# A table of turns for the engines' order up to the spectra, one weight tile loaded from ScalarE's queue, and the last stores of v on two queues

## The chip, the cores and the metric

The kernel runs on one core of one Trainium2 chip. The metric is the device time of one execution in microseconds (us), and lower is better. Engines are named as the profile names them: PE is TensorE, DVE is VectorE, ACT is ScalarE, POOL is GpSimd, and SP is SyncE, which here only issues DMAs. All arithmetic is in float32; where a matmul needs more than one pass allows, its operands are split into a high part (`..h`) and a low part (`..l`).

## The reference

The inputs are a sequence `u` of 2048 rows with 448 channels, the parameters of a diagonal state-space layer (S4D) with 256 modes for each channel, and the three matrices of a gated linear unit (GLU), 448 to 1792 and back. The row normalisation of `u` goes into both branches, and the output is the sum of `u` and the two.

```python
xn  = (u - mean(u)) / sqrt(var(u) + 1e-5)            # per row, L=2048, D=448
# S4D branch: a kernel K[d, l] for each channel, then a convolution of length 2L by FFT
dt  = exp(log_dt);  A = -exp(log_A_real) + 1j*A_imag
C   = (C_real + 1j*C_imag) * dt[:, None]
P   = exp((A*dt[:, None])[:, :, None] * arange(L))   # D x 256 x L
K   = 2 * einsum("dn,dnl->dl", C, P).real
y   = irfft(rfft(xn^T, 2L) * rfft(K, 2L), 2L)[:, :L]^T + xn * D_skip
# GLU branch, F = 1792
g   = (sigmoid(xn @ w_gate) * (xn @ w_up)) @ w_down
out = u + y + g
```

## The kernel before, in words

Two Python generators emit the program, and a driver takes turns between them by shares of planned work, so that the convolution's small operations lie among the GLU's matmuls. `conv()` holds the S4D branch and `glu()` the GLU.

`glu()` works on two halves of 1024 rows, with 14 tiles of 128 hidden columns in groups (`FCH`). For each tile f the weights come by DMA into `wraw` (`w_load`, L646 and L648, six DMAs: for each of two matrices three blocks of 128 rows, and the last 64 rows in two parts). ACT rounds them to `wh` (L763) and DVE takes the rest, `wl` (L767). There is a single buffer `wraw`, so the load of the next tile can start only when both have read it. `gate` makes the products `gu` (PE, L712, four banks of PSUM for `gu`, `po` and others together), `th` on ACT (L720), `hf` on DVE (L723), `hh` on ACT (L728), `hl` on DVE (L730). With `dh` (ACT, L793) and `dl` (POOL, L794) the down product `po` follows on PE (L826), and DVE adds it to `acc` (L831). Some weights are stored for the second half (`wt_d`, `dt_d`, L784).

`conv()` first normalises, makes the first stage of the transform of xn (`x_spec`), and prepares the S4D parameters (`prep`), whose phases it stores to memory (`phu_d`, `phv_d`, `phh_d`, L390). Then comes the kernels' stage, `kgen`, in 56 chunks of 8 channels (the loop variable `cn`). A chunk has these steps:

- `ahead`: phases `ph` are loaded (L489), PE multiplies them out to `tr` (L539), and ACT turns them into cosines and sines `S` (L547 to L550, the last of which, L550, depends on L547).
- `powers`: DVE makes the powers `pm` of the modes' decay, each from the one before it (L453), with three operations of ACT (L446, and L456 twice); a set serves 8 chunks.
- `magnitudes`: POOL spreads the powers to tables `me` and `mf` (L505, L517), and ACT squares part of them (L530).
- DVE multiplies `me` and `mf` with `S` to the factors `Et` (L604 and L605) and `Ft` (L606).
- PE sums the modes, `ko` (L620). After four chunks, ACT copies the sums to `ks` (L633), PE makes the first stage of their transform, `kp` and `kq` (L565), ACT copies these to `sk` (L571) and issues their store to `sk_d` (L572).

After that the spectra: for 17 steps, the kernels' and xn's first stages are loaded (`skl`, `sx`), PE finishes the transforms (`sp`, L912), DVE multiplies them (`yy`), `back` turns the product to `pv` on PE (L939), ACT copies it to `vt` (L945), and SP stores it to `v_d` (L957). `turned` loads it in another order (`vp`, L963), and `last` makes the output (L974). The sums `acc` of the first half go to memory (`acc_d`) and come back as `ac` (L1017).

What sets the order before: the Tile scheduler puts instructions of an engine in order by priority. `tc.high_priority` (called `hp`) moves an operation ahead, and `tc.issue_after(x)` holds one back until x has been placed:

```python
with tc.issue_after(glu_mm[0].ins):       # PE: L285, L434, L620, L565
with tc.issue_after(fts[0].ins) if behind else nullcontext():   # powers: L453, L456
with tc.issue_after(mls[0].ins) if mls else nullcontext():      # magnitudes on POOL
with tc.issue_after(sins[0].ins) if sins else nullcontext():    # squares on ACT
```

Each engine then works through its list strictly in order; a waiting instruction holds up everything behind it.

## Time and profile before

| what | value |
|---|---|
| time, median of 3 runs | 729.61 us (727.99 to 733.26) |
| profiled execution | 730.14 us |
| its span | 728.4 us (1.74 us of the time lie around it) |
| mean granted TensorE clock | 0.978 of full speed |
| instructions in the span | 19114 |

The span runs from the first to the last instruction in the trace, and all positions in the text are counted from its start. Busy shares are means over the span; an engine's idle time has in brackets the instruction or the transfer that ended it. A row of a timeline joins equal instructions that follow one another (`x3`), and its length is then that of all of them. Starts of pipelined instructions overlap the ends of those before them by some tenths of a microsecond.

### The profile page before, as it was taken

The numbers are of one execution on the slowest core, as the hardware profiler recorded it, in microseconds if no ns is written. First come the engines' busy times: TensorE is split into PE (matmuls) and PEld (weight loads), VectorE is DVE, ScalarE is ACT, GpSimd is POOL, SyncE is SP. The second block draws the span as 40 slices with busy tenths as digits, with TensorE's granted clock in tenths as the row PEclk, the third lists the DMA queues.
The fourth block names the chain that finished last, engine by engine and source line by source line (L and its number), as shares of the span: only waits on it lengthen the run. The fifth ranks groups of instructions, "written<-read, shape, count | busy, mean of one in ns | idle before, by whom it ended". The sixth has DMA issues, their size and how long they took to land.

```text
span 728.4 us, 19114 instructions
## 1 busy us (share of the span) xinstructions
PE 682.1 (94%) x7789; PEld 537.9 (74%) x7789; DVE 567.6 (78%) x777; ACT 421.3 (58%) x651; POOL 379.4 (52%) x425
## 2 busy tenths in 40 slices
PE   2997899997998999999999999999999999998996
PEld 1775688786876788666777887888877787776785
DVE  5699997699999999999589988987866555565544
ACT  3645455678677788898397687776742222322320
POOL 2111018699888688788556865776845001351002
PEclk9998899999999999998999999999999999999999
DMA  9936328524414445354853242232269999999845
GB/s 205 233 100 185 103 80 253 170 96 166 161 51 134 168 148 172 99 184 139 247 165 132 59 146 93 73 110 68 74 159 249 287 232 225 236 239 234 189 131 162
DMA packets 92711, 115.72 MB, mean 159 GB/s; under 512 B 12432, under 2 KB 81040, under 8 KB 92368
## 3 DMA queue, kind: packets, MB, share of 16 engines
q1 hardware_dynamic: 83328, 94.15, 47.8%
q10 hardware_dynamic: 6752, 14.69, 6.4%
q0 software_dynamic: 2544, 5.67, 3.2%
q8 instruction: 61, 1.00, 0.6%
q14 instruction: 26, 0.21, 0.1%
HBM read 69.70 MB, written 44.76 MB: 157 GB/s over the span
## 4 chain that ended last, share of the span: by engine, by line
PE 60%; DVE 14%; DMA 11%; ACT 6%; issue 4%; POOL 3%; SPq 2%; ACTq 0%; DVEq 0%; POOLq 0%
PE gu L712 25%; PE po L826 14%; PE ko L620 6%; PE sp L912 5%; PE tr L539 4%; PE pv L939 3%; DVE Ft L606 2%; DVE Et L605 2%; DVE Et L604 2%; DMA acc_d<-acc 1%; DMA tb<-in_c_tab_dram 1%; POOL me L517 1%; DVE hl L730 1%; DMA xe<-in_A_u_dram 1%; DMA sx<-x_d 1%
## 5 line engine op out<-in xcount | busy, mean ns | idle before, releaser
L517 POOL TENSOR_TENSOR me<-me,pm 128x32 f32<-128x32 f32 (+1 forms) x168 | 145.6, 866 | 88.0 <-DVE Et L605 75.5
L517 POOL TENSOR_TENSOR mf<-mf,pm 128x64 f32<-128x64 f32 (+1 forms) x112 | 118.6, 1059 | 4.9
L712 PE MATMUL gu<-xh,wh 128*128 128x512 f32 x336 | 101.9, 410 | 1.4 <-ACT xh L220 1.4
L712 PE MATMUL gu<-xh,wl 128*128 128x512 f32 x336 | 95.7, 392 | 0.0
L712 PE MATMUL gu<-xl,wh 128*128 128x512 f32 x336 | 95.1, 390 | 0.0
L826 PE MATMUL po<-dh,hh 128*128 128x448 f32 (+1 forms) x227 | 87.4, 385 | 4.5 <-DVE acc L831 2.5
L604 DVE TENSOR_TENSOR Et<-me,S 128x1024 f32<-128x1024 f32 x56 | 82.3, 1469 | 9.0 <-ACT S L550 6.7
L605 DVE TENSOR_TENSOR Et<-me,S 128x1024 f32<-128x1024 f32 x56 | 79.5, 1420 | 8.6 <-ACT me L530 8.4
L606 DVE TENSOR_TENSOR Ft<-mf,S 128x1024 f32<-128x1024 f32 x56 | 80.2, 1432 | 7.0 <-ACT S L550 4.3
L826 PE MATMUL po<-dl,hh 128*128 128x448 f32 (+1 forms) x227 | 85.1, 375 | 0.0
L826 PE MATMUL po<-dh,hl 128*128 128x448 f32 (+1 forms) x227 | 84.2, 372 | 0.0
L547 ACT ACTIVATE S<-tr 128x1024 f32<-128x1024 f32 x56 | 57.8, 1032 | 43.5 <-PE tr L539 36.2
L712 PEld LDWEIGHTS gu<-xh,wh 128*128 128x128 f32 x336 | 62.4, 193 | 20.4 <-issue 4.9
L728 ACT CAST hh<-hf 128x512 fp32r<-128x512 f32 x56 | 35.0, 625 | 73.3 <-DVE hf L723 59.6
L620 PEld LDWEIGHTS ko<-Et,Ft 128*32 128x32 f32 x3584 | 54.9, 112 | 27.5 <-issue 17.2
L712 PEld LDWEIGHTS gu<-xh,wl 128*128 128x128 f32 x336 | 63.3, 189 | 15.1 <-DVE pl L313 0.7
L620 PE MATMUL ko<-Et,Ft 128*32 128x64 f32 x3584 | 65.1, 225 | 9.3 <-DVE Ft L606 4.8
L712 PEld LDWEIGHTS gu<-xl,wh 128*128 128x128 f32 x336 | 63.0, 188 | 14.0 <-issue 0.7
L723 DVE SCALAR_TENSOR_TENSOR hf<-th,gu 128x512 f32<-128x512 f32 x56 | 38.1, 680 | 36.8 <-PE gu L712 26.2
L550 ACT ACTIVATE S<-S,hpi 128x1024 f32<-128x1024 f32 x56 | 65.5, 1170 | 0.0
L831 DVE SCALAR_TENSOR_TENSOR acc<-po,acc 128x448 f32<-128x448 f32 (+1 forms) x81 | 48.7, 611 | 21.0 <-PE po L826 21.0
L720 ACT ACTIVATE th<-gu 128x512 f32<-128x512 f32 x56 | 33.7, 601 | 49.2 <-PE gu L712 49.2
(198 smaller groups left out, 1311.1 us busy)
## 6 DMA issues: line engine op xcount, KB each, us to landing
sk_d<-sk ACTq DMA_DIRECT2D x14, 512.0 KB
sx<-x_d SPq DMA_DIRECT2D x32, 224.0 KB
skl<-sk_d SPq DMA_DIRECT2D x16, 448.0 KB
vp<-v_d SPq DMA_DIRECT2D x16, 448.0 KB
v_d<-vt SPq DMA_DIRECT2D x62, 112.0 KB
wt_d<-wh SPq DMA_DIRECT2D x9, 512.0 KB
wt_d<-wl SPq DMA_DIRECT2D x9, 512.0 KB
wl<-wt_d SPq DMA_DIRECT2D x9, 512.0 KB
```

The lines of the kernel that those rows point to most:

```text
L517: ins = nc.gpsimd.tensor_tensor(m[:, :, w + a : 2 * w : n], m[:, :, a:w:n], par(base + i).unsqueeze(2).to_broadcast([128, 4 * DC, w // n]) ...
L547: nc.scalar.activation(rows(cs), pv, AF.Abs)
L550: sins[:] = [nc.scalar.activation(cs, cs, AF.Sin, scale=-TWO_PI, bias=hpi)]
L604: v.tensor_tensor(Et[:, :, :, 32:64], two(me[:, :, 32:64]), S[:, 1::-1], ALU.mult)
L605: v.tensor_tensor(Et[:, :, :, 0:32], two(me[:, :, 0:32]), S[:, 1:3, :, ::-1], ALU.mult)
L606: fts[:] = [v.tensor_tensor(Ft, two(mf), S[:, 3:5], ALU.mult)]
L620: nc.tensor.matmul(ko[32 * j : 32 * j + 32, sl], Ft[:, cc, DC * h + 4 * q + j], Et[:, cc, DC * h + 4 * q + j], start=(k == 0), stop=(k == ...
L712: glu_mm[:] = [nc.tensor.matmul(ps, a_, b_, start=(n == 0), stop=(n == len(mm) - 1))]
L723: marks[1] = v.scalar_tensor_tensor(hf, th, 1.0, pgu[1], ALU.add, ALU.mult)
L826: glu_mm[:] = [nc.tensor.matmul(po[:, ds], a_[:, bs], w_[:, ds], start=(n == 0), stop=(n == 3 * fc - 1))]
L831: v.scalar_tensor_tensor(acc[:, b, ds], po[:, ds], 0.5, acc[:, b, ds], ALU.mult, ALU.add)
L912: mm = nc.tensor.matmul(to, tb[:kk, t, 64 * c : 64 * c + 64], rhs, start=True, stop=True, skip_group_check=True,)
```

## The change

There are three parts.

First, a table `TURNS` holds, for DVE, ACT, POOL and PE, the positions of instructions in the order in which the program emitted them; `0 2 1 3+2` reads: the first, the third, the second, and then two from the fourth on. After all is emitted, `in_turn` chains every instruction of an engine that the table names to the one ahead of it, without a semaphore, so that the scheduler keeps this order. The table ends where the spectra begin (about 300 us into the span). Where the program held an operation back by `issue_after` in that part, the call is now `free`, which does nothing. Second, the load of the GLU's weight tile 7 (issued at f = 6) goes out from ACT's queue in place of SP's. Third, in the very last `back`, DVE copies the second half of `vt`, and the four stores to `v_d` go out two from SP and two from ACT.

```diff
+TURNS = {
+    "DVE": """
+0 2 1 3+2 6 5 7+15 26 30 32 34 36 31 33 22 35 24 37 25 29 38 23 39+13 27 86+2 28 56 52 54+2 58 60 62 64 66 68
...
+def in_turn(tc):
+
+    info = mybir.DependencyInfo(mybir.DependencyClass.NoSync, mybir.DependencyReason.DATA)
+    traced = tc.nc.cur_bb.bb.instructions
+    for name, text in TURNS.items():
+        own = [i for i in traced if i.engine == getattr(mybir.EngineType, name)]
+        turns = []
+        for run in text.split():
+            first, _, n = run.partition("+")
+            turns += own[int(first) : int(first) + int(n or 1)]
+        for one, two in zip(turns, turns[1:]):
+            tc.add_manual_dep(two, one.name, info, reason="in_turn")
...
+    free = lambda ins: nullcontext()
...
-            with tc.issue_after(glu_mm[0].ins):
+            with free(glu_mm[0].ins):
...
-            with tc.issue_after(fts[0].ins) if behind else nullcontext():
+            with free(fts[0].ins) if behind else nullcontext():
...
-            with tc.issue_after(sins[0].ins) if sins else nullcontext():
+            with free(sins[0].ins) if sins else nullcontext():
...
-                                raws.append((w_load(f + 1), None))
+                                raws.append((w_load(f + 1, eng=nc.scalar if f == 6 else nc.sync), None))
...
-                            with hp(HP), tc.issue_after((act if f == 1 else marks)[0].ins):
+                            with hp(HP), free((act if f == 1 else marks)[0].ins):
...
-        def back(h, k, ys_):
+        def back(h, k, ys_, engs=(nc.sync, nc.sync)):
...
-                nc.scalar.copy(vt[:, i], pvs[i])
...
+                if i and engs[0] is not engs[1]:
+                    v.tensor_copy(vt[:, i], pvs[i])
+                else:
+                    nc.scalar.copy(vt[:, i], pvs[i])
+
+            pairs = [(j, i) for j in range(2) for i in range(n)]
+            for j, i in pairs if engs[0] is engs[1] else sorted(pairs, key=lambda p: p[1]):
+                k1 = k + 2 * j + i
...
+                engs[j].dma_start(to.rearrange("r w d -> w r d"), fr)
...
-        back(*prev)
+        back(*prev, (nc.sync, nc.scalar))
...
+    in_turn(tc)
```

The lines of the changed kernel stand 89 lines further down than those of the kernel before in most of the program (L453 is L542 there, L723 is L812, L831 is L920).

How this moves instructions is shown at three places. The first is DVE's order where the kernels' stage opens, about 121 to 134 us into the span of before: `pm0` are the powers, `wl_1601` is the low part of weight tile 7, `hf`, `hl` and `acc` belong to the GLU. Before:

```order
L723 SCALAR_TENSOR_TENSOR hf_1209<-th_1207,gu_1195 128x512
L730 TENSOR_TENSOR hl_1212<-hf_1209,hh_1211 128x512
L453 SCALAR_TENSOR_TENSOR pm0_1132<-W1_110 128x128
L831 SCALAR_TENSOR_TENSOR acc_102<-po_1215,acc_102 128x448
L453 SCALAR_TENSOR_TENSOR pm0_1132<-pm0_1132 128x128 x3
L767 TENSOR_TENSOR wl_1601<-wraw_1413,wh_1600 128x1024
L831 SCALAR_TENSOR_TENSOR acc_102<-po_1226,acc_102 128x448
L453 SCALAR_TENSOR_TENSOR pm0_1132<-pm0_1132 128x128
L831 SCALAR_TENSOR_TENSOR acc_102<-po_1237,acc_102 128x448
L453 SCALAR_TENSOR_TENSOR pm0_1132<-pm0_1132 128x128 x3
L831 SCALAR_TENSOR_TENSOR acc_102<-po_1248,acc_102 128x448
```

After the change, the same place:

```order
L812 SCALAR_TENSOR_TENSOR hf_1209<-th_1207,gu_1195 128x512
L542 SCALAR_TENSOR_TENSOR pm0_1132<-W1_110 128x128
L819 TENSOR_TENSOR hl_1212<-hf_1209,hh_1211 128x512
L920 SCALAR_TENSOR_TENSOR acc_102<-po_1215,acc_102 128x448
L542 SCALAR_TENSOR_TENSOR pm0_1132<-pm0_1132 128x128 x6
L856 TENSOR_TENSOR wl_1601<-wraw_1413,wh_1600 128x1024
L542 SCALAR_TENSOR_TENSOR pm0_1132<-pm0_1132 128x128 x2
L920 SCALAR_TENSOR_TENSOR acc_102<-po_1226,acc_102 128x448
L542 SCALAR_TENSOR_TENSOR pm0_1132<-pm0_1132 128x128
L920 SCALAR_TENSOR_TENSOR acc_102<-po_1237,acc_102 128x448
L920 SCALAR_TENSOR_TENSOR acc_102<-po_1248,acc_102 128x448
```

Seven of the ten powers now stand ahead of `wl_1601`, where four stood, and the other three are through one or two additions earlier.

The second place is ACT's order at the same time: `th` and `hh` are the GLU's, `GG_111` takes the prepared C, `pm0` is the powers' tile, and `wraw_1413` and `wh_1600` are weight tile 7. Before:

```order
L720 ACTIVATE th_1207<-gu_1183 128x512
L728 CAST hh_1211<-hf_1209 128x512
L436 COPY GG_111<-ko_1040 128x2x14x8
L436 COPY GG_111<-kp_1044 128x2x14x8
L446 ACTIVATE pm0_1132<-W1_110,one_74 128x128
L763 CAST wh_1600<-wraw_1413 128x1024
L456 ACTIVATE pm0_1132<-pm0_1132,one_74 128x640 x2
```

After the change:

```order
L809 ACTIVATE th_1207<-gu_1183 128x512
L535 ACTIVATE pm0_1132<-W1_110,one_74 128x128
L735 DMA wraw_1413<-in_B_w_gate_dram 128x3x128
L817 CAST hh_1211<-hf_1209 128x512
L525 COPY GG_111<-ko_1040 128x2x14x8
L737 DMA wraw_1413<-in_B_w_gate_dram 64x128
L525 COPY GG_111<-kp_1044 128x2x14x8
L737 DMA wraw_1413<-in_B_w_gate_dram 64x128
L735 DMA wraw_1413<-in_B_w_up_dram 128x3x128
L737 DMA wraw_1413<-in_B_w_up_dram 64x128 x2
L852 CAST wh_1600<-wraw_1413 128x1024
L545 ACTIVATE pm0_1132<-pm0_1132,one_74 128x640 x2
```

The powers' first operation now stands ahead of `hh_1211` and of both copies to `GG_111`, and the six DMAs of the weight load, which stood among the stores of `phv_d` and `phh_d` on SP's queue, lie between these.

The third place is ACT's order in the kernels' stage, at a copy `ks` of the modes' sums (about 172 us into the span of before). Before:

```order
L720 ACTIVATE th_2581<-gu_2525 128x512
L793 CAST dh_2593<-rd_2594 128x448
L530 ACTIVATE me0_1131<-me0_1131 128x32x16
L728 CAST hh_2585<-hf_2583 128x512
L633 COPY ks_1122<-ko_2067 128x512
L547 ACTIVATE S1_1125<-tr_2409 128x2x2x256
L548 ACTIVATE S1_1125<-tr_2409 128x2x2x256
L549 ACTIVATE S1_1125<-tr_2409 128x512
L720 ACTIVATE th_2729<-gu_2624 128x512
```

After the change:

```order
L809 ACTIVATE th_2581<-gu_2525 128x512
L882 CAST dh_2593<-rd_2594 128x448
L722 COPY ks_1122<-ko_2067 128x512
L636 ACTIVATE S1_1125<-tr_2409 128x2x2x256
L637 ACTIVATE S1_1125<-tr_2409 128x2x2x256
L817 CAST hh_2585<-hf_2583 128x512
L638 ACTIVATE S1_1125<-tr_2409 128x512
L639 ACTIVATE S1_1125<-S1_1125,hpi_72 128x2x512
L809 ACTIVATE th_2729<-gu_2624 128x512
```

The copy `ks` and two of the sines now stand ahead of `hh_2585`. PE's order in that stage has the kernels' chunks `ko` up to five GLU matmuls earlier, `tr` and `kp` up to eight; from about 310 us on DVE, ACT, POOL and PE have the order of before. On SP, besides the six DMAs, the four loads of `ac` (L1017) stand together ahead of two loads of the spectra (`skl`, `sx`), and the load of `t32` stands one place earlier.

More of the change, by code (lines that the diff above doesn't have):

```diff
@@ L54 @@
 NCH = 8
+TURNS = {
+    "DVE": """
[18 rows of a table added]
+""",
+    "Activation": """
[15 rows of a table added]
+""",
+    "Pool": """
[8 rows of a table added]
+""",
+    "PE": """
[22 rows of a table added]
+""",
+}
+def in_turn(tc):
[9 more added lines that the diff above has]
+            tc.add_manual_dep(two, one.name, info, reason="in_turn")
 def _tables():
@@ L430, in turn @@
             ps = psc[-1].tile([128, 2, 128], F32, name=("ko", "kp")[t], bufs=1)
-            with tc.issue_after(glu_mm[0].ins):
+            with free(glu_mm[0].ins):
                 for k in range(2):
@@ L444, in powers @@
         pm = pms[g % 2]
-        with tc.issue_after(behind.ins) if behind else nullcontext():
+        with free(behind.ins) if behind else nullcontext():
             nc.scalar.activation(pm[:, 0], w, AF.Identity, bias=one)
@@ L502, in magnitudes @@
             gg = GGs[0][:, 2 * b : 2 * b + 2].rearrange("p c h e -> p (c h e)")
-            with tc.issue_after(mls[0].ins) if mls else nullcontext():
+            with free(mls[0].ins) if mls else nullcontext():
                 nc.gpsimd.tensor_tensor(
@@ L515, in magnitudes @@
                     a, n = (1, 2) if m is me and i > 3 else (0, 1)
-                    with tc.issue_after(mls[0].ins) if mls else nullcontext():
+                    with free(mls[0].ins) if mls else nullcontext():
                         ins = nc.gpsimd.tensor_tensor(
@@ L613, in kgen @@
                     ko = psc[-1].tile([128, 8, 64], F32, name="ko", bufs=1)
-                with tc.issue_after(glu_mm[0].ins):
+                with free(glu_mm[0].ins):
                     for q in range(2):
@@ L635, in kgen @@
                 if cn % 4 == 2 and cn > 3 or cn + 1 == NCK:
-                    with hp(HP) if cn + 1 == NCK else tc.issue_after(glu_mm[0].ins):
+                    with hp(HP) if cn + 1 == NCK else free(glu_mm[0].ins):
                         first_stage((cn - 3) // 4 if cn + 1 < NCK else cn // 4)
@@ L676, in pair_norm @@
     def pair_norm(b, xns):
-        with hp(HP), tc.issue_after(marks[0].ins), tc.issue_after(marks[1].ins):
+        with hp(HP), free(marks[0].ins), free(marks[1].ins):
             for i in range(2):
@@ L1075, in conv @@
                     with hp(HP):
-                        with tc.issue_after(normed.ins) if q else nullcontext():
+                        with free(normed.ins) if q else nullcontext():
                             for b in range(4 * q, 4 * q + 4):
@@ L1094, in conv @@
                 preps = [prep(pst, h, srcs[h]) for h in range(2)]
-                with tc.issue_after(xls[0].ins):
+                with free(xls[0].ins):
                     for b in range(8):
@@ L1110, in conv @@
                         try:
-                            with tc.issue_after(hfs[max(0, len(hfs) - LAG)].ins):
+                            with free(hfs[max(0, len(hfs) - LAG)].ins):
                                 next(p)
```

16 lines of the change are left out of this document (6 added, 10 removed), and 62 rows, old and new, of the table TURNS.

## The prediction, before the changed kernel had run

> **What bounds the kernel now.** I read the page first, for the engines' shares, then the busy times by stretch, then the waits inside the stretch that the change rearranges, then the timelines at its two ends.
>
> ```profile
> PE 682.1 (94%) x7789; PEld 537.9 (74%) x7789; DVE 567.6 (78%) x777; ACT 421.3 (58%) x651; POOL 379.4 (52%) x425
> ```
>
> TensorE (PE) is busy for 94% of the span, so the 46 us in which it is not are nearly all that an order can win. The shares hide stages with different limits, which the next view separates. Its columns are the stretch, its length, the busy time of PE, PEld, DVE, ACT and POOL, the granted clock, the DMA share and GB/s.
>
> ```profile
> 120.00:140.00 20.00, 18.28 (x90) 16.20 (x89) 9.70 (x21) 8.32 (x14) 9.97 (x18) 1.00 0.74 233
> 140.00:300.00 160.00, 151.20 (x2203) 122.42 (x2202) 152.76 (x152) 125.60 (x183) 135.76 (x134) 0.98 0.39 130
> 345.00:545.00 200.00, 196.92 (x3003) 161.97 (x2998) 163.85 (x170) 139.43 (x202) 133.34 (x154) 1.00 0.39 121
> 545.00:680.00 135.00, 132.57 (x1033) 99.66 (x1033) 75.56 (x144) 37.48 (x72) 31.87 (x37) 1.00 1.03 243
> ```
>
> From 140 to 300 us VectorE (DVE) works 152.76 of 160 us and PE 151.20: the two run neck and neck, and PE has 8.8 us to give. From 345 on PE is busy for 98%, so what the kernel gains before 300 us is carried to the end rather than swallowed by a later wait; from 545 to 680 the DMA engines are full as well (1.03), and the bytes are the same in both kernels. The waits from 138 to 300 us (engine and line <- what ended the wait: us in total, times, longest) say what holds PE in that stage, and what holds DVE:
>
> ```profile
> PE ko L620 <- DVE Ft L606: 3.1, 4, 1.9
> PE ko L620 <- DVE Et L604: 2.9, 1, 2.9
> PE kp L565 <- ACT ks L633: 1.9, 2, 1.0
> ```
>
> ```profile
> DVE Et L604 <- ACT S L550: 3.2, 2, 2.2
> DVE Et L605 <- ACT me L530: 2.2, 5, 0.6
> ```
>
> PE loses 7.9 us to the kernels' factors (Et, Ft) and to the copy of their sums (ks). Those products come late because DVE is full, and DVE itself loses only 5.4 us to ScalarE (ACT) work that is late. An order can take away such waits; it can't shorten DVE's 152.76 us.
>
> **The opening (term 1).** The kernels' chain starts here with the powers pm on DVE (L453). The next two views are DVE's and ACT's timelines (start, us, operation, and in brackets the idle time before it and what ended it):
>
> ```profile
> 124.32 0.93 DVE L453 SCALAR_TENSOR_TENSOR pm<-pm 128x128 f32<-128x128 f32 x3
> 130.29 1.23 DVE L767 TENSOR_TENSOR wl<-wraw,wh 128x1024 fp32r<-128x1024 f32 x1 [5.04 <-ACT wh L763]
> 131.44 0.62 DVE L831 SCALAR_TENSOR_TENSOR acc<-po,acc 128x448 f32<-128x448 f32 x1
> ...
> 134.09 0.86 DVE L453 SCALAR_TENSOR_TENSOR pm<-pm 128x128 f32<-128x128 f32 x2
> ...
> 140.11 1.23 DVE L604 TENSOR_TENSOR Et<-me,S 128x1024 f32<-128x1024 f32 x1 [2.20 <-ACT S L550]
> ```
>
> ```profile
> 123.32 0.41 ACT L446 ACTIVATE pm<-W,one 128x128 f32<-128x128 f32 x1
> 129.21 1.05 ACT L763 CAST wh<-wraw 128x1024 fp32r<-128x1024 f32 x1 [5.48 <-DMA ph<-phu_d]
> 133.02 0.83 ACT L456 ACTIVATE pm<-pm,one 128x640 f32<-128x640 f32 x1 [2.76 <-DVE pm L453]
> 134.98 0.83 ACT L456 ACTIVATE pm<-pm,one 128x640 f32<-128x640 f32 x1 [1.13 <-DVE pm L453]
> ...
> 138.86 1.16 ACT L550 ACTIVATE S<-S,hpi 128x1024 f32<-128x1024 f32 x1
> ```
>
> Before, DVE does four powers (the last three in the first row), sits 5.04 us behind wl (which waits for wh, and wh for the loaded weights), and then does the last six among the acc additions. ACT's two `one`-additions (L456) wait for these, and the sines behind them (the last is L550) set the first Et at 140.11. After, three more powers, seven in all, stand ahead of wl. The six that the first L456 needs lie in the 5.04 us of idle time, so that it starts when wh ends, 129.21 + 1.05 = 130.26, not at 133.02. The second L456 needs the three that are left: wl ends at 130.29 + 1.23 = 131.52, two powers take 0.86, the acc addition that stands among them 0.62, the last power half of 0.86: 133.43 against 134.98, 1.55 earlier. From there the chain to L550 and Et has the same instructions, so **term 1 is -1.5 us**. What is late next: the chain's first tr, of which PE's timeline says:
>
> ```profile
> 132.90 0.70 PE L539 MATMUL tr<-sel,ph 128*128 128x512 f32 x2 [1.72 <-DMA ph<-phv_d]
> ```
>
> It ends at 133.60, and in the new order the first sine wants it at about 134.5 (133.43, plus 0.83 for L456 and a short square), so this wait doesn't come to bind. That PE idle time of 1.72 us I count as not won: the next po matmuls need banks that the acc additions free, and these now stand behind wl and two powers.
>
> The new ACT order puts a wait here. pm's first operation (L446), which stood behind hh and the two copies of GG, now stands ahead of them, and it overwrites memory that a store of the parameters still reads (fr to phv_d). SP's timeline gives that store and the weight load of tile 7, which moves to ACT's queue:
>
> ```profile
> 118.98 0.96 SPq L390 DMA_DIRECT2D phv_d<-fr  x1
> ...
> 125.89 1.18 SPq L648 DMA_DIRECT2D wraw<-in_B_w_up_dram  x2
> ```
>
> The store has landed no earlier than its issue ends, 119.94, and no later than 123.32, where L446 ran before without a wait; between these I take 122.5, near the later end, since the stores issued ahead of it share the DMA engines. Queued behind it on ACT are hh, both GG copies, and the six issues of the load. hh is wanted by the po matmuls, of which PE has work to 131, so a delay of a microsecond costs nothing while that queue of matmuls lasts. The six issues at 1.18 / 2 = 0.59 us are 3.5 us, and lie in the 5.48 us that ACT idles ahead of wh; from 122.5, with L446, hh and GG (about 1.7 us together) between, the last goes out at about 127.7, against 125.89 + 1.18 = 127.07. On the other side SP no longer carries these six, so the parameters' stores and the phase loads behind them go out up to 3.5 us earlier; that is the tr that doesn't bind. The bounds of term 1: +0.8 when the weights land as late as their later issue and wh is pushed (127.7 - 127.07 = 0.6, and a little), -2.2 when Et's whole wait of 2.20 goes. I take -1.5, which is worked out and not a bound.
>
> **140 to 300 us (term 2).** In this stage the table exchanges neighbours. On DVE the three factor products stand one or two places ahead of hf, hl, acc or wl; on ACT the sines go ahead of hh, th or dh, and ks copies too; PE's ko chunks move up by at most five GLU matmuls and the two kinds kp and tr by at most eight. No instruction is added or removed, DVE stays full, and whatever the kernels' products gain the GLU's hf and hl lose. PE has about as much of the one as of the other, so I count the exchange of DVE's order as nothing; what covers it is the GLU matmuls that PE can do while it waits for Et, and PE's waits for hf or hl take over where these run out. The ks copies are a real gain: ACT is not full (125.60 of 160), and a copy that no longer stands behind hh and dh frees PE's kp matmuls at once. Of the two waits of 1.9 us in all I take the shorter, 1.9 - 1.0 = 0.9, since the longer may be a copy that can't start before ko ends. **Term 2 is -0.9 us**, bounds -5.4 (all of DVE's waits for ACT go) and +4.0 (the slower rival below).
>
> **The end (term 3).** ACT copies the last two results vt, SP issues four stores and the load of vp, and PE waits for it; ACT's, SP's, DVE's and PE's timelines, in turn:
>
> ```profile
> 704.05 0.97 ACT L945 COPY vt<-pv 128x448 f32<-128x448 f32 x2 [3.89 <-PE pv L939]
> ```
>
> ```profile
> 704.61 2.46 SPq L957 DMA_DIRECT2D v_d<-vt  x4
> 708.66 0.53 SPq L963 DMA_DIRECT2D vp<-v_d  x1
> ```
>
> ```profile
> 706.11 0.62 DVE L831 SCALAR_TENSOR_TENSOR acc<-po,acc 128x448 f32<-128x448 f32 x1 [3.01 <-PE po L826]
> ```
>
> ```profile
> 713.45 0.80 PE L974 MATMUL pv<-vp,wf 64*32 64x224 f32 x24 [1.79 <-DMA out_dram<-acc]
> ```
>
> Four issues in 2.46 us are 0.61 each. In pairs on two queues the last ends two issues, 1.2 us, sooner. The second copy goes to DVE, which idles 3.01 us there, and runs beside the first; that takes half of 0.97 off the start of the second pair, but their queue is then set by the first pair, so I count nothing for it. PE waits 1.79 us for this chain (the label names the last transfer seen, but between the stores and the matmuls only the load of vp is left), more than 1.2, so **term 3 is -1.2 us**, bounds 0 and -1.8. The Trainium skill ("DMA: Bandwidth & Descriptors", section "Issuing engines are not separate DMA queues") says that issuing from several engines saves only the issue time, usually small beside the transfer. By that remark term 3 would be near nothing and the sum about 727.7; the row of four issues, 2.46 us ahead of a load that starts 1.6 us after them, speaks for the 1.2.
>
> SP's other moves, the four loads of the sums acc_d that now stand together ahead of two loads of the spectra, and t32 one place earlier, I cost at zero: the same bytes in a stretch where the DMA share is 1.03 anyway. If the spectra's load is late by a place there, a microsecond may be lost; it lies inside the range.
>
> **The rivals.**
>
> A, the exchanges pay more. If ACT's sines, moved ahead, take away both of DVE's waits, 5.4 us in place of 0.9 are won: 730.14 - 1.5 - 5.4 - 1.2 = 722.0. For it: DVE is the fullest engine there, so its idle time is the kernel's. Against it: five of these seven waits are for the squares me (L530), at most 0.6 each, which hang on POOL's chain.
>
> B, the clock. Two rows of PE's timeline and two by stretch:
>
> ```profile
> 177.32 1.86 PE L620 MATMUL ko<-Et,Ft 128*32 128x64 f32 x64 [2.95 <-DVE Et L604]
> 235.20 1.73 PE L620 MATMUL ko<-Et,Ft 128*32 128x64 f32 x64 [1.90 <-DVE Ft L606]
> ```
>
> ```profile
> 176.00:180.00 4.00, 2.68 (x66) 2.44 (x67) 4.00 (x6) 2.19 (x4) 3.84 (x3) 0.68 0.37 115
> 236.00:240.00 4.00, 4.00 (x81) 2.98 (x74) 3.97 (x5) 3.22 (x5) 1.50 (x2) 0.64 0.40 128
> ```
>
> After PE's two longest waits the granted clock was 0.68 and 0.64 over 4 us: 0.32 x 4 + 0.36 x 4 = 2.7 us of PE's time. If the new order shortens both waits so that the dips stay out, the time is 726.5 - 2.7 = 723.8. For it: Et and Ft are what these waits are for, and they move up. Against it: at both places DVE is full (4.00 and 3.97), and moving one wait may open another. The Trainium skill ("TensorE: Matmul & The Clock Gate", section "What's actually happening") states that the clock halves after an idle window of about 3.4 us whose windows run free; both waits here are shorter, so by its letter neither need have dipped, and the trace decides that they did.
>
> C, slower. The factors go ahead, and the GLU's hf goes behind Ft; hh on ACT then slips behind the sines or in between them, and pushes the last sine (L550), for which the next Et waits. DVE's and ACT's timelines show the place:
>
> ```profile
> 216.42 1.87 DVE L606 TENSOR_TENSOR Ft<-mf,S 128x1024 f32<-128x1024 f32 x1
> ...
> 220.54 2.10 DVE L604 TENSOR_TENSOR Et<-me,S 128x1024 f32<-128x1024 f32 x1 [1.01 <-ACT S L550]
> ```
>
> ```profile
> 219.35 1.16 ACT L550 ACTIVATE S<-S,hpi 128x1024 f32<-128x1024 f32 x1
> ```
>
> L550 ends at 220.51, and Et starts at once: here ACT sets DVE's pace already. If hf starts behind Ft, 1.87 later, and about half of this, 1.0 us, reaches L550, four places of this kind cost 4.0. With nothing won in the opening: 730.14 + 4.0 - 1.2 = 732.9. It decides from the point where the delay of hf is more than the slack of the sines behind it. Against it: ACT has 34 us free in this stage.
>
> D, hidden. The opening's gain ends in a wait for wl or for the GLU's banks, the exchanges cancel, and only the end pays: 730.14 - 1.2 = 728.9. That ends so too if the table by and large repeats the order that the chip already follows.
>
> **How the numbers follow.** The sum goes by the profiled execution, span 728.4 and 1.74 around it: 730.14 - 1.5 - 0.9 - 1.2 = **726.5**. That execution lies 0.5 above the median of the three runs, and the forecast is 0.4% under that median, within the 1% that a measurement of this kernel can tell from no change. Chances: forecast 0.43, A 0.13, B 0.16, C 0.15, D 0.13. The range goes from 720.5 (A with the far bounds of terms 1 and 3 is 730.14 - 2.2 - 5.4 - 1.8 = 720.7) to 733.0 (C), which leaves out half of A's and C's spread and some of the rest. 1% below the median is 722.3: most of A, a little of B and of the forecast lie there, 0.18. 1% above is 736.9: only a C twice as dear, 0.04. Within: 0.78.
>
> **What would show it.** Term 1: the first L456 right after wh, the second near 133.4, the first Et near 138.6, while wh still starts near 129.2. Term 2: PE's 1.9 us for ks shrinks while the sum of its waits for Et and Ft stays near 6. Term 3: two v_d issues on each queue, vp's load about 1.2 us sooner after the copies, PE's last wait about 0.6. In B the clock stays at 1.00 through the stage. In C, DVE's waits for L550 grow from 3.2 towards 7 us. I am wrong if the waits of PE in the kernels' stage fall or rise by more than 3 us, or if the DMA-bound stretch after 545 changes its length.

## The result: slower by 1.2%, and the profile after

The changed kernel takes 737.16 us (median of 14 runs, 732.81 to 741.48) against 729.22 us for the kernel before on the same chips: a ratio of 1.0116, 95% interval 1.0093 to 1.0139. The forecast was 726.5 us with a range of 720.5 to 733.0, and it gave what came a chance of 0.04. The profiled execution (span 731.0 us) is the shortest of the 14, and its PE is 2.1 us ahead of the kernel before at 119 us, where the orders are still the same; what follows leans on the experiments for sizes and on the trace for places.

Two statements ahead of the prediction have to be put right. The table goes on to the end of the kernels' stage at some 540 us (its orders differ from those of before up to about 310, ACT's up to 322), and the load of t32 moved ahead on SP's queue by five places, not one: past two loads of `dl`, two of `dh` and the second store of `acc_d`.

The busy times by stretch, columns as before:

```profile
120.00:140.00 20.00, 15.75 (x70) 13.61 (x69) 8.86 (x21) 8.42 (x13) 9.20 (x21) 0.91 0.63 200
140.00:300.00 160.00, 150.47 (x2194) 120.94 (x2192) 147.36 (x149) 123.18 (x177) 124.85 (x127) 1.00 0.40 128
345.00:545.00 200.00, 195.52 (x2939) 160.40 (x2935) 164.10 (x169) 138.43 (x200) 133.78 (x155) 0.99 0.40 122
545.00:680.00 135.00, 133.16 (x1087) 100.95 (x1084) 76.29 (x145) 38.62 (x73) 35.11 (x41) 1.00 0.99 240
```

In the opening PE works 15.75 of 20 us, not 18.28. From 140 to 300 us DVE, the engine that was to stay full, is busy for 147.36 us, not 152.76. The waits from 138 to 300 us, PE's and then DVE's, say why:

```profile
PE ko L709 <- DVE Ft L695: 5.0, 3, 1.9
PE ko L709 <- DVE Et L693: 2.3, 1, 2.3
PE kp L654 <- ACT ks L722: 1.0, 1, 1.0
```

```profile
DVE Et L694 <- ACT me L619: 5.0, 5, 1.5
...
DVE Et L694 <- POOL mf L606: 2.3, 1, 2.3
DVE Et L693 <- ACT S L639: 2.1, 2, 1.8
DVE wl L856 <- ACT wh L852: 1.3, 2, 1.1
```

DVE's two waits for ACT that were to shrink (5.4 us for S and the squares me) are 7.1, its wait for POOL's mf has grown from 0.5 to 2.3, and one for wh has joined them (the row left out is a wait of 3.0 for PE, at the end of the opening). PE loses 7.3 us to Et and Ft where it lost 6.0; only its wait for ks went down, from 1.9 to 1.0, the 0.9 of term 2.

The opening: DVE, ACT with the loads from its queue, and PE.

```profile
131.41 1.23 DVE L856 TENSOR_TENSOR wl<-wraw,wh 128x1024 fp32r<-128x1024 f32 x1 [6.69 <-ACT wh L852]
```

```profile
122.99 0.50 ACTq L737 DMA_DIRECT2D wraw<-in_B_w_gate_dram  x1
126.12 0.40 ACTq L735 DMA_DIRECT2D wraw<-in_B_w_up_dram  x1
127.41 1.14 ACTq L737 DMA_DIRECT2D wraw<-in_B_w_up_dram  x2
130.33 1.04 ACT L852 CAST wh<-wraw 128x1024 fp32r<-128x1024 f32 x1 [7.71 <-DMA wraw<-in_B_w_up_dram]
131.28 0.82 ACT L545 ACTIVATE pm<-pm,one 128x640 f32<-128x640 f32 x1
134.21 0.83 ACT L545 ACTIVATE pm<-pm,one 128x640 f32<-128x640 f32 x1 [2.10 <-DVE pm L542]
```

```profile
134.03 0.74 PE L915 MATMUL po<-dh,hh 128*128 128x448 f32 x1 [3.59 <-DVE acc L920]
```

The third of the issues ends at 123.49 and the next starts at 126.12, 2.6 us later, where 0.59 from one to the next was assumed. The weights land at 130.3, wl is done at 132.64, and the acc addition behind wl and two powers holds PE for 3.59 us. The clock fell after that wait: it is 0.91 in the first row of the table of stretches where it was 1.00, which is 1.8 of the 20 us, and the po matmuls from 134.0 to 136.8 us took 0.57 us each and not 0.37.

Since the order up to 120 us is the same in both kernels on every engine, one can follow single instructions: the start of the same gu or po matmul, after less before, is -2.1 us at 119 us, +2.1 at 142, -2.7 at 242, +2.2 at 277, +2.1 at 359, +5.0 at 379, +4.7 at 545, +3.1 at 690 and +2.4 at 720. The opening loses 4.2; the stage wins 4.8 up to 242 us and loses 4.9 by 277; another 2.9 go at 359 to 379, behind the end of the orders' differences on all engines but SP. Nearly all of the 4.8 is won at the two places where the clock dipped before: from 172 to 188 and from 228 to 244 us it was 0.89 before and is 1.00 after, 3.5 us together. The place from 359 to 379 is ACT's:

```profile
368.63 0.62 ACT L817 CAST hh<-hf 128x512 fp32r<-128x512 f32 x1 [7.12 <-DMA acc_d<-acc]
```

Here the row of before, and then SP's queue after and before:

```profile
364.62 0.62 ACT L728 CAST hh<-hf 128x512 fp32r<-128x512 f32 x1 [4.04 <-DMA acc_d<-acc]
```

```profile
355.04 0.35 SPq L1085 DMA_DIRECT2D t<-in_c_t_dram  x1
355.48 0.38 SPq L894 DMA_DIRECT2D dl<-dt_d  x1
355.92 0.46 SPq L894 DMA_DIRECT2D dh<-dt_d  x1
357.88 0.32 SPq L935 DMA_DIRECT2D acc_d<-acc  x1
```

```profile
352.05 0.34 SPq L805 DMA_DIRECT2D dl<-dt_d  x1
352.48 0.39 SPq L805 DMA_DIRECT2D dh<-dt_d  x1
353.52 0.32 SPq L846 DMA_DIRECT2D acc_d<-acc  x1
```

The acc tile was ready at 353.49 us before (the row of its last addition: 352.87 and 0.62) and its store went out at once; after, it was ready at 355.60 (354.98 and 0.62) and the store went out 2.3 us later. Of these, 0.8 us went by behind t32, dl and dh; the other 1.5 the store waited itself, by the profile for a load of acc, and why is not shown. ACT's next loads of acc overwrite what this store reads; they go out some 10 us behind it in both traces, and hh waits behind them. At the head of the queue t32's load waits for the stores of the first stage of x, as the load of dl did before (waits of SP from 345 to 366 us, after and before):

```profile
SPq L1085 <- DMA x_d<-x: 10.1, 2, 9.5
```

```profile
SPq L805 <- DMA x_d<-x: 6.1, 1, 6.1
```

The end did roughly what was said, PE's last wait falling from 1.79 to 1.03 us:

```profile
715.75 2.52 PE L1065 MATMUL pv<-vp,wf 64*32 64x224 f32 x76 [1.03 <-DMA out_dram<-acc]
```

### The profile page after: what moved, and what is told of

Its sections match the earlier page's. It is cut to its first block, busy times and chain, and to the rows that moved or that the text cites. A ratio compares the mean times of both kernels' runs of the same rounds, so it can differ in the third digit from the quotient of the medians.

```text
span 731.0 us, 19124 instructions
## 1 busy us (share of the span) xinstructions
PE 677.3 (93%) x7789; PEld 532.2 (73%) x7789; DVE 564.8 (77%) x778; ACT 422.1 (58%) x650; POOL 373.4 (51%) x425
## 4 chain that ended last, share of the span: by engine, by line
PE 47%; DVE 5%; DMA 2%; ACT 2%; issue 1%; ACTq 1%; DVEq 0%; SPq 0%
PE gu L801 17%; PE po L915 10%; PE sp L1001 7%; PE pv L1028 4%; PE ko L709 4%; PE tr L628 2%; DVE Ft L695 1%; DMA acc_d<-acc 1%; PE pv L1065 1%; DVE Et L693 1%; PE kp L654 1%; DVE Et L694 1%; ACTq L786 1%; PE kq L654 1%; DMA acc<-in_A_u_dram 1%
## 5 line engine op out<-in xcount | busy, mean ns | idle before, releaser
L606 POOL TENSOR_TENSOR me<-me,pm 128x32 f32<-128x32 f32 (+1 forms) x168 | 136.6, 813 | 98.4 <-DVE Et L694 87.6
L606 POOL TENSOR_TENSOR mf<-mf,pm 128x64 f32<-128x64 f32 (+1 forms) x112 | 124.9, 1115 | 4.9
L693 DVE TENSOR_TENSOR Et<-me,S 128x1024 f32<-128x1024 f32 x56 | 83.0, 1483 | 6.7 <-ACT S L639 5.2
L694 DVE TENSOR_TENSOR Et<-me,S 128x1024 f32<-128x1024 f32 x56 | 77.1, 1377 | 12.7 <-ACT me L619 10.3
L812 DVE SCALAR_TENSOR_TENSOR hf<-th,gu 128x512 f32<-128x512 f32 x56 | 38.2, 682 | 37.2 <-PE gu L801 31.1
L920 DVE SCALAR_TENSOR_TENSOR acc<-po,acc 128x448 f32<-128x448 f32 (+1 forms) x81 | 48.4, 609 | 19.4 <-PE po L915 19.3
L915 PEld LDWEIGHTS po<-dh,hh 128*128 128x128 f32 x227 | 44.2, 195 | 21.5 <-DVE acc L920 7.3
```

The lines of the kernel that those rows point to most:

```text
L606: ins = nc.gpsimd.tensor_tensor(m[:, :, w + a : 2 * w : n], m[:, :, a:w:n], par(base + i).unsqueeze(2).to_broadcast([128, 4 * DC, w // n]) ...
L693: v.tensor_tensor(Et[:, :, :, 32:64], two(me[:, :, 32:64]), S[:, 1::-1], ALU.mult)
L694: v.tensor_tensor(Et[:, :, :, 0:32], two(me[:, :, 0:32]), S[:, 1:3, :, ::-1], ALU.mult)
L812: marks[1] = v.scalar_tensor_tensor(hf, th, 1.0, pgu[1], ALU.add, ALU.mult)
L915: glu_mm[:] = [nc.tensor.matmul(po[:, ds], a_[:, bs], w_[:, ds], start=(n == 0), stop=(n == 3 * fc - 1))]
L920: v.scalar_tensor_tensor(acc[:, b, ds], po[:, ds], 0.5, acc[:, b, ds], ALU.mult, ALU.add)
```

## The experiments

The program of the changed kernel was kept, and its table rewritten, with a part for SP added. Each engine's order is cut where both kernels have placed the same set of instructions: at 138 us (end of the "opening"), 225 us (end of the "early" part of the kernels' stage) and 320 us (end of its "late" part). A stretch takes its order from the changed kernel or from before; the queue of weight tile 7's load goes with the opening, unless it is said otherwise. The opening changes the orders of DVE, ACT and SP, the early part those of all engines, the late part those of all but POOL. All ratios are to executions of the kernel before beside those of the run, 12 of each run (late_act 6).

**One part put back into the changed kernel.**

```diff
 # t32_back: TURNS["SP"], the six instructions from t32 on
-t32, dl, dh, acc_d, dh, dl
+dl, dh, acc_d, dh, dl, t32
 # opening_back: all engines up to 138 us as before, and
-raws.append((w_load(f + 1, eng=nc.scalar if f == 6 else nc.sync), None))
+raws.append((w_load(f + 1), None))
 # middle_back: all engines from 138 to 320 us as before
```

> The changed kernel with one thing put back: the load of t32 (L1085 there) stands on SP's queue where it stood before, behind the second store of acc_d and four loads of dt_d, no longer ahead of them. In the changed kernel's profile ACT waits 7.12 us for that store to land before it can issue the next loads of acc, and hh stands behind these; before it waited 4.04. Theory 1 (the change's losses lie in three places: the opening about 4 us, t32 about 3, the rest near nothing): this kernel takes 737.2 - 3 = 734 us, and ACT's wait is near 4. Theory 2 (the order of the kernels' stage is what costs; waits behind it are absorbed): 737, unchanged.

> The changed kernel with the opening put back: on all engines the order up to about 138 us, and the queue of weight tile 7's load, are those of before; all behind it is as changed. Theory 1: PE no longer waits 3.6 us for acc behind wl, the time is 737.2 - 4 = 733 us. Theory 2: what PE wins it loses again to the kernels' chain, which starts no earlier: about 737.

> The changed kernel with the kernels' stage put back: from about 138 us to 320 us the order of DVE, ACT, POOL, PE and SP is that of before; opening, t32, the loads of ac and the end are as changed. Theory 1: in the two profiles PE is 4.8 us ahead at 245 us and has lost 4.9 by 270, so the stage costs nothing: 737 us. Theory 2: DVE's waits from 138 to 310 us, which grew from about 10 to 17 us, are the loss: 731 to 733.

Measured: t32_back 735.64 us, ratio 1.0101 (1.0070 to 1.0133); opening_back 731.68, 1.0045 (1.0016 to 1.0075); middle_back 729.29, 1.0011 (0.9983 to 1.0040). Theory 1 falls: it took the stage for free because PE had won and lost the same in one trace, yet putting the stage back wins the most, 1.05% of 1.16%. Theory 2 falls at opening_back, for which it said 737 us. Putting back the opening wins 0.7%, t32 0.15%, which these intervals can't tell from nothing. The three sum to 1.9%, more than there is to win; added up, their intervals are about as wide as the excess. That some losses exist only together is therefore a guess here, which a later table bears out for two stretches.

The trace of t32_back also speaks against reading ACT's longer wait as t32's: with t32 back ACT waits 7.21 us ahead of hh, where near 4 was expected. Over the 14 traces in which t32 stands as before and ACT's loads have not been moved this wait is 3.8 to 7.2 us, and the store goes out up to 1.4 us behind its tile; in the four with t32 ahead it is 7.1 to 7.9, and 1.8 to 2.3. So t32 makes the store late, but a step like that from 4.04 to 7.12 comes without it too.

**One part alone.** end_only has all orders of before and the change in `back`; the others add one stretch to it.

```diff
 # end_only: order of before everywhere, one load queue as before, and
-        back(*prev)
+        back(*prev, (nc.sync, nc.scalar))
 # t32_only: end_only with t32 ahead on SP;  opening_only: with the opening
 # middle_early_only: with 138 to 225 us;  middle_late_only: with 225 to 320 us
```

> The kernel before with the last edit alone: the last two v_d stores go out from ACT's queue and the second copy of vt is DVE's. Both theories: in the changed profile the last wait shrank by 0.8 us, so 729.2 - 0.8 = 728.4. If the split saves nothing because the transfer decides: 729.2.

> The kernel with the end's edit alone (727.1 us), and t32's load moved ahead on SP's queue to where the changed kernel has it. Theory 1 (four losses that add up: opening, late part of the kernels' stage, t32, and little else): the second store of acc_d lands some 3 us later, ACT holds hh for 7 to 8 us rather than 3.8, and the time is 729 to 730 us. Theory 2 (the moved load only matters for an engine that is behind already): 727, with the wait of 7 us in the trace all the same.

> The kernel with the end's edit alone (727.1 us), and the opening as changed: all engines' order up to 138 us and weight tile 7's load on ACT's queue. Theory 1: PE waits some 4 us for acc behind wl where it waited 1.7 for ph, and catches up a part of it by 210 us: 729 to 730 us. Theory 2 (PE catches up all, since DVE's chain is what bounds from 140 us on): 727.

> The kernel with the end's edit alone (727.1 us), and the kernels' stage as changed from 138 to 225 us only. Theory 1: the changed order gains here (PE is 3 us further on at 210 us in the profiles) or does nothing: 725 to 727 us. Theory 2 (the loss is spread evenly over the stage, since the squares me stand behind more on ACT): 729.5.

> The kernel with the end's edit alone (727.1 us), and the kernels' stage as changed from 225 to 320 us only. Theory 1: here the loss lies; DVE waits 2.2 us for POOL's mf near 240 and 1.1 for wh near 256 with hf and hl queued behind, and the time is 730 to 732 us. Theory 2 (spread evenly): 729.5.

| kernel | median us | ratio to before | interval |
|---|---|---|---|
| end_only | 727.11 | 0.9973 | 0.9944 to 1.0001 |
| t32_only | 731.96 | 1.0024 | 0.9988 to 1.0059 |
| opening_only | 725.78 | 0.9947 | 0.9919 to 0.9976 |
| middle_early_only | 727.24 | 0.9962 | 0.9927 to 0.9997 |
| middle_late_only | 732.01 | 1.0036 | 1.0001 to 1.0071 |

Against end_only the late part costs 0.63%, as theory 1 had it (the two intervals just meet), and t32 0.5%, where the intervals overlap; the early part costs nothing. The opening alone is no loss either: PE loses its 3.6 us for acc there too (the same matmuls are 4.4 us later from 131 to 140 us), and has won 5.1 back by 210. Of these it wins 3.9 at one place, 172 to 178 us: in end_only PE waits there 1.00 us for ks and 2.94 for Et, and the clock is 0.89 from 172 to 188 us; in opening_only, where PE comes later, it waits 1.25 in all, and the clock is 1.00. opening_only has the lowest median of all runs and is faster than the changed kernel by 1.7%. Its interval lies below the kernel before, as do those of middle_early_only and of opening_sp below; none of the three can be told from end_only, which all of them contain.

**The late part, engine by engine.** Here only one engine has the changed order, from 225 to 320 us; opening_and_early joins the two stretches that cost nothing alone.

```diff
 # late_pe, late_dve, late_act: end_only, from 225 to 320 us
-TURNS[engine] as before
+TURNS[engine] as changed      # one of "PE", "DVE", "Activation"
 # opening_and_early: end_only with the opening and 138 to 225 us as changed
```

> The kernel with the end's edit alone (727.1 us), and from 225 to 320 us PE's order as changed (ko, tr and kp ahead of up to eight GLU matmuls), with DVE, ACT, POOL and SP as before. Theory P (the stage's late part, 732.0 us, loses because PE comes to ko before its factors are there, and the GLU matmuls that would cover the wait now stand behind): 730 to 732 us, with PE waits for Ft of over 1 us near 250 and 267. Theory D (DVE and ACT lose the time, PE only shows it): 727 to 728.

> The kernel with the end's edit alone (727.1 us), and from 225 to 320 us DVE's order as changed (Et and Ft ahead of hf, hl, wl), the other engines as before. Theory P: 727 or less, since the factors come earlier and PE has its cover. Theory D: 730 to 732 us, since hf and hl stand behind factors that wait for POOL and ACT.

> The kernel with the end's edit alone (727.1 us), and from 225 to 320 us ACT's order as changed (sines ahead of hh, th, dh, wh), the other engines as before. Theory P: 727. Theory D: part of the loss, 728 to 730 us, through wh and hh, for which wl and hl on DVE wait.

> The changed orders that cost nothing by themselves, together: opening (with weight tile 7 on ACT's queue) and kernels' stage from 138 to 225 us as changed, the end's edit; from 225 us on, t32 and the loads of ac as before. If the two gains add up (725.8 and 727.2 alone, against 727.1 with the end's edit only): 725.9 us, between 724 and 727, under the kernel before by 0.4 to 0.6%. If the opening's delay of PE is only caught up because the stage behind it has before's order: 728 to 730.

late_pe takes 727.58 us (0.9987, 0.9958 to 1.0015), late_dve 732.90 (1.0063, 1.0035 to 1.0090), late_act 733.13 (1.0061, 1.0037 to 1.0085). Theory P falls: PE's order costs nothing that can be measured, and DVE's or ACT's by itself costs as much as all together (SP's turn of that part was not run by itself). DVE's timeline of end_only, and of late_dve at the same place:

```profile
226.56 1.43 DVE L705 TENSOR_TENSOR Ft<-mf,S 128x1024 f32<-128x1024 f32 x1
227.92 0.72 DVE L552 SCALAR_TENSOR_TENSOR pm<-pm 128x128 f32<-128x128 f32 x1
228.56 0.68 DVE L829 TENSOR_TENSOR hl<-hf,hh 128x512 fp32r<-128x512 f32 x1
229.86 2.10 DVE L704 TENSOR_TENSOR Et<-me,S 128x1024 f32<-128x1024 f32 x1 [0.62 <-ACT me L629]
231.89 0.67 DVE L822 SCALAR_TENSOR_TENSOR hf<-th,gu 128x512 f32<-128x512 f32 x1
```

```profile
229.94 1.29 DVE L704 TENSOR_TENSOR Et<-me,S 128x1024 f32<-128x1024 f32 x1 [2.88 <-ACT me L629]
231.16 0.90 DVE L829 TENSOR_TENSOR hl<-hf,hh 128x512 fp32r<-128x512 f32 x1
```

Before, Ft, a power and hl fill the time until the square me is ready. With Et moved ahead of them, DVE stands for 2.88 us, and hl, whose hh was there, stands behind it. And late_act, DVE and then ACT:

```profile
226.20 0.68 DVE L822 SCALAR_TENSOR_TENSOR hf<-th,gu 128x512 f32<-128x512 f32 x1
...
230.41 0.94 DVE L829 TENSOR_TENSOR hl<-hf,hh 128x512 fp32r<-128x512 f32 x1 [2.40 <-ACT hh L827]
```

```profile
228.85 1.02 ACT L647 ACTIVATE S<-tr 128x1024 f32<-128x1024 f32 x1
229.76 0.62 ACT L827 CAST hh<-hf 128x512 fp32r<-128x512 f32 x1
```

hf was done at 226.88, but hh comes behind ks and two sines, and DVE waits 2.40 us for it. What reaches PE of this are these waits, in end_only, in late_dve and in late_act:

```profile
233.75 0.27 PE L664 MATMUL kp<-wk,ks 64*64 64x64 f32 x1 [0.63 <-ACT ks L732]
...
236.23 1.31 PE L719 MATMUL ko<-Et,Ft 128*32 128x64 f32 x64 [1.90 <-DVE Ft L705]
```

```profile
235.41 0.27 PE L664 MATMUL kp<-wk,ks 64*64 64x64 f32 x1 [3.56 <-ACT ks L732]
...
259.21 0.47 PE L925 MATMUL po<-dh,hl 128*128 128x448 f32 x1 [1.60 <-DVE hl L829]
```

```profile
233.07 1.76 PE L719 MATMUL ko<-Et,Ft 128*32 128x64 f32 x64 [3.73 <-DVE Ft L705]
...
265.35 1.10 PE L719 MATMUL ko<-Et,Ft 128*32 128x64 f32 x64 [2.46 <-DVE Ft L705]
```

In late_dve hf stands behind the Et that waits; hh on ACT comes behind this late hf, ks behind hh, and PE stands for ks (at 259.2 for an hl that stands behind Ft). In late_act Ft stands behind the hl that waits. So it is not the GLU alone that pays: an exchange that was to bring the kernels' products forward holds up their own chain. With both orders changed DVE waits at other places: in middle_late_only 2.24 us for POOL's mf at 241.7 and 1.08 for wh at 258.6.

opening_and_early takes 731.73 us (1.0040, 1.0017 to 1.0063), where 725.9 was the sum. In its trace PE is 5.9 us later from 131 to 140 us and has won back 3.2 by 210, not 5.1 as in opening_only, and it loses 2.9 more from 296 to 350.

**Which half of the opening.** The order without the queue, the queue without the order, each without and with the early part:

```diff
 # opening_sp: opening_only, and          opening_sp_early: the same, 138 to 225 us as changed
-raws.append((w_load(f + 1, eng=nc.scalar if f == 6 else nc.sync), None))
+raws.append((w_load(f + 1), None))
 # opening_queue: end_only, and           opening_queue_early: the same, 138 to 225 us as changed
-raws.append((w_load(f + 1), None))
+raws.append((w_load(f + 1, eng=nc.scalar if f == 6 else nc.sync), None))
```

> Beside the end's edit, the opening's new order with weight tile 7 still loaded from SP's queue. Theory Q (ACT's queue makes the tile late, and this late tile is what holds PE 3.6 us for acc): wl starts near where it did before, PE's wait is about 1 us, and the time is 724 to 726 us. Theory O (the order does it, acc behind wl and powers): PE waits over 3 us all the same; 726 to 728.

> Beside the end's edit, weight tile 7 loaded from ACT's queue with the opening's order as before. Theory Q: wl is 2 to 4 us late and PE is held at acc or at the next gate for about as long; 727 to 729 us. Theory O: PE's wait is that of before, 1 to 2 us; 726 to 727.

> As the run with the opening's new order and SP's queue, with the early part of the kernels' stage as changed. Theory Q: with PE no longer behind at 140 us, the early order costs nothing: 725 to 727 us. Theory O: 731, as with ACT's queue.

> As the run with ACT's queue and the opening's old order, with the early part of the kernels' stage as changed. Theory Q: PE is behind at 140 us and the early order doesn't let it catch up: 730 to 732 us. Theory O: 727.

| opening | stage as before | early part as changed |
|---|---|---|
| as before | 0.9973 (0.9944 to 1.0001) | 0.9962 (0.9927 to 0.9997) |
| order only | 0.9961 (0.9928 to 0.9995) | 1.0020 (0.9991 to 1.0050) |
| queue only | 1.0042 (1.0006 to 1.0078) | 1.0016 (0.9983 to 1.0048) |
| both | 0.9947 (0.9919 to 0.9976) | 1.0040 (1.0017 to 1.0063) |

Neither theory fits the table. The queue alone costs (733.51 us, more than theory Q said), but with the new order it does not. The early part costs 0.9% after the whole new opening; after its order alone 0.6%, though there the intervals just overlap; it costs nothing after the queue alone and after the old opening. PE's waits from 122 to 142 us are 4.7 us with the queue alone, 3.7 with the order alone, 3.6 with both, and 1.0 in end_only, so each half by itself makes PE stand.

Part of what passes from the opening to the early part can be read off the traces, at 170 to 180 us, where opening_only won its loss back. With the stage as before PE waits there 3.8 to 4.2 us in the eight traces with the old opening, 1.2 to 1.5 in the four with its new order, and 2.4 with the queue alone. With the early part as changed it waits 2.9 to 3.0 without the new order and 1.9 to 3.3 with it: the place where the opening's delay was absorbed has little left to absorb. That is some 2 us; the rest of the 0.9% is not shown, and stays open.

**How t32 costs.** ACT's four loads of the second acc tile stand behind the next two hh, in the run with t32 ahead and in the fastest one:

```diff
 # t32_loads_later (on t32_only), opening_loads_later (on opening_only): TURNS["Activation"]
-acc load, acc load, hh, acc load, acc load, me, ... hh
+hh, me, ... hh, acc load, acc load, acc load, acc load
```

> The run with t32's load moved ahead (732.0 us), and ACT's four loads of the second acc tile moved behind the next two hh, so that hh no longer waits for the store of acc_d. If ACT's wait is how t32's load costs its time: 727 to 728 us, as with the end's edit alone, and no ACT wait of 7 us ahead of hh. If it costs by the late dl and dh loads behind it on SP's queue: 731 to 732, and PE waits for dl or dh between 355 and 400 us.

> The run with the opening as changed and the end's edit (725.8 us, the fastest so far), with the same four loads moved. There ACT waits 4.8 us for the store, but PE loses only 0.8 us between 366 and 382: 725 us, no measurable gain.

t32_loads_later takes 729.20 us, 1.0000 (0.9974 to 1.0026), half way between the two expectations, and its interval overlaps those of t32_only and of end_only. ACT's wait of 7.9 us in t32_only is gone, and with it DVE's 6.0 for hh, but DVE now waits longer ahead of hf (in t32_only 4.1 us). Its waits from 355 to 400 us:

```profile
DVE hf L822 <- PE gu L811: 8.5, 3, 4.0
DVE Ft L705 <- PE ko L719: 2.6, 2, 2.3
DVE hf L822 <- issue: 2.6, 1, 2.6
```

opening_loads_later takes 730.12 us, 1.0009 (0.9987 to 1.0031), slower than opening_only by 0.6% where nothing was expected. So moving the loads costs something of its own, and whether the hold of hh is all of t32's cost can't be settled from these runs.

## Why the prediction was wrong

**Term 2 failed, and with it the sign.** It said of the stage: "whatever the kernels' products gain the GLU's hf and hl lose. PE has about as much of the one as of the other, so I count the exchange of DVE's order as nothing". An exchange on an engine that works in order is only neutral if what moves ahead is ready. Et and Ft were not: they need squares from ACT and tables from POOL, and DVE stood with ready GLU work behind. The late part alone costs 0.63%, some 4.6 us, and DVE's order or ACT's alone as much; putting the whole stage back takes 1.05%, 7.7 us, off the changed kernel. Both lie beyond the right end of term 2's bounds (-5.4 to +4.0). The reading behind the term was short as well: the waits of before have a row "DVE Et L604 <- ACT me L530: 1.0, 1, 1.0" that it left out, so DVE lost 6.4 us to ACT there and not 5.4. The sign named for an error, PE's waits in the stage moving by more than 3 us, did not come: in the profiles they went from 8.2 to 9.4, while the clock there rose from 0.98 to 1.00.

**Rival C had the sign and half of the mechanism.** hh did slip in between the sines, but DVE's hl waited for it (2.40 us in late_act), not the next Et for L550: DVE's waits for that fell from 3.2 to 2.1 us where C had them grow. Its four places at 1.0 us were a guess; single waits were 1.1 to 2.9 us. Its "point from which it decides", the slack of the sines, wasn't looked up: the squares me stand behind th, dh and the sines on ACT, and this could be read off the rows of before (waits "DVE Et L605 <- ACT me L530", five of them).

**Term 1 failed too, and what looks like its success is luck.** The second L456 came at 134.21 (forecast 133.4, before 134.98) and the first Et at 139.97 (forecast 138.6, before 140.11). But this trace was 2.1 us ahead at 119 us; counted from there the second L456 came 1.3 us later than before, and Et 2.0. The step that failed is the six issues "at 1.18 / 2 = 0.59 us": the fourth of them came 2.6 us late, and wh, on which the chain hangs, started at 130.33, 3.2 us later than before by the same count. ACT's queue is not the only way to that: in opening_sp, which loads from SP, wh is 2.6 us late by this count. Et then stood behind two acc additions that waited for PE. And the wait "not won", acc behind wl, grew from 1.72 us (for ph) to 3.59, with the fall of the clock behind it. All the same opening_only is 0.26% below end_only, which these intervals can't tell from nothing or from the -1.5 forecast; it gets there by PE's shorter wait at 177 us, of which term 1 says nothing.

**Term 3**, -1.2 us, was 0.8 in the trace; end_only measures -0.27% (-0.56 to 0.01), or -2.0 us with an interval of 4 us. The wait shrank, as the row of four issues said; the time by itself can't tell it from nothing.

**SP's moves at zero** rested on a misreading: t32 moved by five places and not by one, and the store of acc_d behind it went out late. Its cost is 0.5% in t32_only and 0.15% in t32_back, neither of them clear of nothing. The loads of `ac` that now stand together were not run by themselves; in the profile nothing is lost behind 545 us, where they lie.

**Rival B** had its mechanism and not its time. In the profile of after, the clock from 140 to 300 us is 1.00 as B had it, but it fell in the opening, and over all runs the mean granted clock of the changed kernel is 0.980 and that of the kernel before 0.979, while the time rose. A and D, which had the time fall or stay, are out with it.

## What to carry to other kernels

Before moving an operation ahead on an in-order engine, look up in the trace when its last operand is ready, on each engine that feeds it; what moves ahead of ready work and waits turns the whole queue behind it into idle time. A table that fixes four engines leaves the fifth to the scheduler: read its queue too, entry by entry, since a load that waits at its head holds the stores behind it. Stretches that each cost nothing can cost together, so an order is measured whole, and in parts only to learn where it loses.

## What the runs showed of the hardware

Executions of one kernel spread by some 5 to 12 us here, and part of this is the clock: within a kernel, the time falls by 4.1 us for each 0.01 of mean granted clock (worked out over all runs; correlations of -0.4 to -0.9). The Trainium skill ("TensorE: Matmul & The Clock Gate", section "What's actually happening") says that the window which decides on the clock runs free, so that each execution meets it elsewhere; the spread agrees with that, and no run here shows the window itself.

The clock followed PE's waits in the opening. In the ten traces with the changed opening or a half of it, PE waits 3.4 to 5.0 us in all between 122 and 142 us, and the clock from 120 to 140 us is 0.83 to 0.96; in the other ten it waits 1.0 to 2.2, and the clock is 1.00. One long wait is not needed for it: in opening_sp_early there are two of 1.84 and 1.57 us, and the clock is 0.83.

Where two kernels have the same order up to 120 us, PE stood up to 5 us apart at 131 us in single traces (late_pe against middle_early_only, which are 4.1 apart at 60 us already), so a single pair of traces can't size a change of this kernel below that, unless it is counted from a place ahead of the change.
